# A place of its own for the mixed tokens of the keys, and an earlier mixture for batch 0

## The chip, the cores and the metric

The kernel runs on one core of a Trainium2 chip. Its time is the device time of one execution, in microseconds. The profile comes from one execution that the hardware profiler recorded.

## The reference

Three layers follow each other, all in float32, for 4 batches of 576 tokens.

1. Attention with 8 heads of 64 columns. The scores are causal; beside q.k/8 they get a bias from s: with cum the running sum of max(s, 0), query i and key j get min(cum[j] - cum[i], 0). Then softmax, and the product with v.
2. A feed-forward layer on the attention's output x (512 columns), with token mixing:

```python
xk = mu_k * x + (1.0 - mu_k) * x_prev      # x_prev: the token before
xr = mu_r * x + (1.0 - mu_r) * x_prev
k = np.maximum(xk @ w_k, 0.0)              # 512 -> 1024
v = k * k @ w_v                            # 1024 -> 512
r = 1.0 / (1.0 + np.exp(-(xr @ w_r)))
x = r * v
```

3. A token and channel mixer with w_tok1, w_tok2, w_ch1 and w_ch2, whose weights and work begin late in the kernel; the change does not touch it.

The weights come in float64.

## The kernel before, in words

**Products.** Most products are made from pairs: each operand is split in a high part, a float32 copy rounded to the faster matrix format, and a low part, the rest. `products` then issues three matrix products for each piece of 128 rows (high x high, high x low, low x high). Tokens and weights all have such pairs.

**Weights.** A float64 weight is loaded as two 32-bit words. `weight_split` (lines 567 to 577) rebuilds a float32 from them with two ScalarE steps (a copy of the high words, an integer scaling of the low ones) and two VectorE steps (shift-or, and-or); ScalarE then copies the high part into the weight's tile, and the low part is a subtraction, on GpSimd for w_k and w_r, on VectorE for w_v. For w_v (half=1) another ScalarE pass multiplies the float32 by 0.5 in place, ahead of the copy: the gate is made as 0.5 (1 + tanh), and this half is put into the weight. The first twelve pieces are w_k (8) and w_r (4), each of 512 KB; their raw tiles come from the pool `wst` (five buffers). w_v comes in 16 pieces of 256 KB, whose raw tiles are borrowed from the six buffers of `xt`, the pool of the attention's outputs.

**Attention of batch 0.** The first 256 queries of each head are done by `early` (two tiles of 128 queries per head, lines 311 to 340), the rest by `late` (three tiles, lines 358 to 385) and `late_pv`. A step is: scores on TensorE, the negated row maximum on VectorE (L261), the exponential on ScalarE (L271), normalising on GpSimd (L274), transposes on TensorE, a copy of them on ScalarE, the product with v. After every second head, the outputs of the pair of heads are copied into `xt[0, p]` by VectorE (line 340). Between the early tiles and in the first late heads `keep_busy` issues products whose result nobody uses; their PSUM tile is one of the two of the pool that `up` uses as well. Batches 1 to 3 follow as visits (`scores`, `transposes`, `values`).

**The feed-forward layer.** `mix(b, c, i, p)` (lines 472 to 481) mixes the tokens of chunk c (0: the first 256, 1: the other 320) for one pair of heads: a scaled copy into a temporary (L478), the other token added (L479), both on VectorE, the high part on ScalarE (L480), the low part on VectorE (L481). i=0 writes XK, i=1 XR. `up` (lines 483 to 493) makes one of eight blocks of k from XK and w_k, then relu and two squares on ScalarE into a temporary and into KK, and the low part on GpSimd (L493). `gate` reads XR, `down` reads KK.

**What sets the order.** Nothing is issued in program order. Each block of code has a place, a number given by `at(place)`; smaller places go first. A planner simulates the engines and writes for each engine a fixed list: whenever an engine is free, the instruction that is ready and has the smallest place. On the chip each engine takes its list in order and waits where something is not ready. The SP, ACT and GpSimd queues also issue the DMAs, in the same manner. Early head h, tile j has place 2h + j; the n-th late step has 16 + n; a feed-forward unit that belongs to step n has 16 + n + 3. The twelve weight splits have places 1.6, 2.8 and so on to 14.8, the w_v pieces 18, 19.5 and so on. The mixes of batch 0's first chunk for XK have place 16, and the mu loads (`mixes`) place 9.

**Memory.** Pools on the left side lie like a stack. First `wst` (raw weight tiles) and `cp` (the early heads' inputs, tiles and the bias) are opened; after both are closed in the program, `act` (XK, XR, KK) and `sm` (the temporaries t and e, three each) take the same memory. A tile may be written once all tiles that lay there before are no longer used. `bias_rows` (lines 164 to 180) makes the running sum of s into `cum`; `split_bias` (lines 182 to 193) writes it, split in pairs, to DRAM (ext_d) in three chunks through one tile `e`; `late_load` reads it back for the late heads.

## Time and profile before

| | |
|---|---|
| time, median of 3 runs | 890.04 us (888.98 to 893.41) |
| the profiled execution | 887.59 us, of which the span is 885.8 us |
| TensorE (PE) busy in the span | 847.3 us |
| VectorE (DVE), ScalarE (ACT), GpSimd (POOL) busy | 535.2, 469.8, 347.9 us |
| mean granted clock of TensorE | 0.982 of full speed |

Times in the rows are microseconds from the start of the span. PE is the matrix product, PEld the load of its stationary operand; L110 is line 110 of the kernel. A busy engine is one that has an instruction in it. "Out <- in" names the tiles. In the views of waits the left side waited for the right one. A granted clock of 1.00 is 2.4 GHz, 0.50 is 1.2 GHz.

### The profile page before, as it was taken

To read this page: it belongs to the slowest core of one execution; us is meant where nothing else is said; L and a number is where in the kernel's file an instruction comes from. 1 tells how busy PE (TensorE), PEld (TensorE's weight loads), DVE (VectorE), ACT (ScalarE), POOL (GpSimd) and SP (SyncE) were. 2 spreads that over 40 slices of the span, in tenths; PEclk is the share of its full clock that TensorE was granted. 3 is DMA by queue.
4 is the path that set the end of the run, shared out by engine and by line. 5 is a ranking of instruction groups with operands and counts; after the bars stand their busy time and mean duration, and the time that the engine had idled before them with its cause. 6 is when DMAs were issued, how large, how long until landed. Compare 5 with 4: busy or idle time off the path is not lost.

```text
span 885.8 us, 17817 instructions
## 1 busy us (share of the span) xinstructions
PE 847.3 (96%) x6185; PEld 793.4 (90%) x6185; DVE 535.2 (60%) x1583; ACT 469.8 (53%) x1320; POOL 347.9 (39%) x510
## 2 busy tenths in 40 slices
PE   7969999999789999999989899999999999999998
PEld 5736677998679999999989899899999999999998
DVE  4896897677899677996657866871331322222321
ACT  3877976866776765868456775760320211211210
POOL 3676876877773433645244674650000000000000
PEclk8969999999999999999999999999999999999999
DMA  7975667578753334441132656653022112112100
GB/s 195 255 207 170 205 188 215 163 215 245 199 159 85 82 79 107 100 121 48 50 100 80 206 157 197 208 186 124 25 71 63 44 40 66 38 42 67 43 25 24
DMA packets 78730, 108.37 MB, mean 122 GB/s; under 512 B 11072, under 2 KB 59200, under 8 KB 78640
## 3 DMA queue, kind: packets, MB, share of 16 engines
q1 hardware_dynamic: 68352, 77.40, 32.0%
q0 software_dynamic: 8416, 29.24, 10.2%
q8 instruction: 49, 0.80, 0.4%
q10 hardware_dynamic: 1872, 0.59, 0.4%
q14 instruction: 41, 0.34, 0.1%
HBM read 77.74 MB, written 28.90 MB: 120 GB/s over the span
## 4 chain that ended last, share of the span: by engine, by line
PE 70%; DVE 9%; DMA 7%; ACT 5%; issue 4%; POOL 3%; SPq 0%; ACTq 0%; POOLq 0%; DVEq 0%
PE c L110 32%; PE vd L110 8%; PE h L110 7%; PE r L110 4%; PE t L110 3%; PE t L411 3%; PE pv L463 3%; DMA hl_d<-qkp 2%; DMA raw<-in_moe_w_ch_dram 2%; DVE raw L572 2%; PE s L286 2%; PE pv L397 2%; PE s L287 2%; DVE raw L573 1%; PE s L368 1%
## 5 line engine op out<-in xcount | busy, mean ns | idle before, releaser
L813 ACT ACTIVATE HID<-c 128x256 fp32r<-128x256 f32 (+1 forms) x96 | 39.4, 410 | 218.7 <-PE c L110 218.5
L274 POOL TENSOR_SCALAR P<-P,sum 64x576 f32<-64x576 f32 (+4 forms) x160 | 101.2, 636 | 94.1 <-DVE sum L273 41.9
L110 PE MATMUL h<-XK,WK 128*128 128x256 f32 (+1 forms) x768 | 124.5, 302 | 4.1 <-ACT k L490 2.0
L110 PE MATMUL vd<-KK,WV 128*128 128x256 f32 (+1 forms) x768 | 121.6, 300 | 0.0
L110 PEld LDWEIGHTS h<-XK,WK 128*128 128x128 f32 x768 | 106.6, 188 | 10.1 <-ACT k L490 3.1
L271 ACT ACTIVATE P<-P,mx 64x576 f32<-64x576 f32 (+4 forms) x160 | 95.9, 600 | 28.5 <-DVE mx L261 27.5
L110 PEld LDWEIGHTS vd<-KK,WV 128*128 128x128 f32 x768 | 106.8, 188 | 1.7 <-issue 0.7
L110 PE MATMUL c<-U,WK 128*128 128x256 f32 (+1 forms) x768 | 102.6, 291 | 2.1 <-DVE HID L814 2.1
L110 PE MATMUL c<-HID,WV 128*128 128x256 f32 (+1 forms) x768 | 104.4, 291 | 0.0
L110 PEld LDWEIGHTS c<-U,WK 128*128 128x128 f32 x768 | 98.7, 188 | 2.4 <-DVE HID L814 2.3
L110 PEld LDWEIGHTS c<-HID,WV 128*128 128x128 f32 x768 | 100.4, 188 | 0.0
L814 DVE SCALAR_TENSOR_TENSOR HID<-c,HID 128x256 fp32r<-128x256 f32 (+1 forms) x96 | 43.9, 457 | 83.3 <-ACT HID L813 83.2
L878 DVE TENSOR_TENSOR ut<-c,ut 128x256 f32<-128x256 f32 (+1 forms) x32 | 14.7, 458 | 119.9 <-PE c L110 112.5
L261 DVE CUSTOM_DVE_ANT_0 P<-s,maskc 64x288 f32<-64x288 f32 (+4 forms) x160 | 74.9, 474 | 16.9 <-PE idle L155 4.4
L493 POOL TENSOR_TENSOR KK<-k,KK 128x256 fp32r<-128x256 f32 (+1 forms) x64 | 53.5, 837 | 34.7 <-ACT k L492 29.2
L110 PE MATMUL r<-XR,WR 128*128 128x320 f32 (+1 forms) x384 | 61.4, 302 | 2.6 <-ACT k L490 2.6
L75 ACT ACTIVATE raw<-raw 128x256 f32<-128x256 f32 (+2 forms) x101 | 46.8, 466 | 29.4 <-DMA raw<-in_moe_w_ch_dram 9.7
L572 DVE SCALAR_TENSOR_TENSOR raw<-raw 128x256 int32<-128x256 int32 (+2 forms) x85 | 49.7, 584 | 19.8 <-ACT raw L571 16.6
L110 PEld LDWEIGHTS r<-XR,WR 128*128 128x128 f32 x384 | 53.9, 192 | 3.6 <-ACT k L490 2.9
L411 PE MATMUL t<-ident,P 128*128 128x128 f32 (+1 forms) x360 | 52.8, 262 | 3.5 <-DVE PT L440 2.4
L110 PE MATMUL c<-HID,WR 128*128 128x256 f32 (+1 forms) x384 | 54.5, 291 | 0.0
L573 DVE SCALAR_TENSOR_TENSOR raw<-raw 128x256 int32<-128x256 int32 (+2 forms) x85 | 52.9, 624 | 1.2
(116 smaller groups left out, 1695.9 us busy)
## 6 DMA issues: line engine op xcount, KB each, us to landing
X<-hl_d SPq DMA_DIRECT2D x72, 288.0 KB
hl_d<-qkp POOLq DMA_DIRECT2D x48, 288.0 KB, 4.2
raw<-in_moe_w_ch_dram POOLq DMA_DIRECT2D x48, 256.0 KB, 3.7
qkr<-in_qk_dram SPq DMA_DIRECT2D x48, 144.0 KB
yt<-y_d SPq DMA_DIRECT2D x16, 288.0 KB
u_d<-yt SPq DMA_DIRECT2D x16, 288.0 KB
raw<-in_moe_w_k_dram SPq DMA_DIRECT2D x8, 512.0 KB
raw<-in_moe_w_v_dram SPq DMA_DIRECT2D x16, 256.0 KB
```

The costliest lines, as they stand in the source:

```text
L75: nc.scalar.activation(out=out, in_=in_, func=AF.Copy, scale=scale)
L110: nc.tensor.matmul(ps, a, b, start=first and i == 0, stop=last and i == n - 1)
L261: nc.vector.tensor_tensor_reduce(out=P[0:m, c0:c1], in0=ps[0:m, 0:c1 - c0], in1=maskc[0:m, 512 - q0 + c0:512 - q0 + c1], scale=-scale, sca ...
L271: nc.scalar.activation(out=P[0:m, 0:w], in_=P[0:m, 0:w], func=AF.Exp, bias=mx[0:m, x:x + 1], scale=-1.0, accum_out=sm[0:m, 0:1])
L274: nc.gpsimd.tensor_scalar(out=P[0:m, 0:w], in0=P[0:m, 0:w], scalar1=sm[0:m, 1:2], scalar2=1.0, op0=ALU.mult, op1=ALU.mult)
L411: nc.tensor.transpose(ps[0:r, p0 + m * k:p0 + m * k + m], P[0:m, 128 * k:128 * k + r], ident[0:m, 0:m])
L463: nc.tensor.matmul(ps[:, o:n], vv[:, k, :], part, start=(k == 0 and t == 0), stop=(k == nk - 1 and t == len(parts) - 1),)
L493: nc.gpsimd.tensor_tensor(out=kk[:, 1, m, 0:n], in0=t[:, 0:n], in1=f32(kk[:, 0, m, 0:n]), op=ALU.subtract)
L572: nc.vector.scalar_tensor_tensor(out=low, in0=high, scalar=3, in1=low, op0=ALU.logical_shift_left, op1=ALU.bitwise_or)
L573: nc.vector.scalar_tensor_tensor(out=low, in0=high, scalar=-2 ** 31, in1=low, op0=ALU.bitwise_and, op1=ALU.bitwise_or)
L813: nc.scalar.activation(out=hi, in_=ps, func=AF.Relu)
L814: nc.vector.scalar_tensor_tensor(out=lo, in0=ps, scalar=0.0, in1=f32(hi), op0=ALU.max, op1=ALU.subtract)
```

## The change

XK gets a pool of its own, opened ahead of `wst`, so that it shares memory with nothing. To make room, `wst` has three buffers and not five, `cum` is computed in place of `st`, and the bias goes to DRAM in four chunks of 144 columns and not three of 192. The four mixes of batch 0's first chunk for XK are placed behind the early heads 1, 3, 5 and 7 (places 3.9, 7.9, 11.9 and 15.9) and use one temporary of 256 columns in `cp`; the mu loads get place 3. The in-place half of w_v is gone: the copy of the high part multiplies by 0.5, and the low part is one VectorE step, 0.5 times the float32 less the high part.

```diff
--- before.py
+++ after.py
@@ -165,7 +165,7 @@
         st = cp.tile([G, S], F32, name="st")
         nc.sync.dma_start(out=st, in_=s)
         e32 = cp.tile([G, 2, 2, QC], F32, name="e32")
-        cum = cp.tile([G, S], F32, name="cum")
+        cum = st
         nc.gpsimd.memset(e32[:, 0, 0, :], 1.0)
         nc.gpsimd.memset(e32[:, 1, 1, :], 1.0)
         for c, (a, z) in enumerate(CHS):
@@ -180,7 +180,7 @@
         return cum, e32
 
     def split_bias(cp, cum):
-        n = 3
+        n = 4
         for c in range(n):
             a, z = S * c // n, S * (c + 1) // n
             e = cp.tile([G, 4, 2, z - a], F32R, name="e")
@@ -474,7 +474,7 @@
         x = xt[b, p]
         a, z = CHS[c]
         n = z - a
-        t = act["sm"].tile([128, CM], F32, tag="t", name="t", bufs=3)
+        t = act["mt"].tile([128, act["mtw"]], F32, tag="t", name="t", bufs=act["mtb"])
         nc.vector.tensor_scalar(out=t[:, 0:n], in0=x[:, 1 + a:1 + z], scalar1=mu[:, i, p:p + 1], scalar2=1.0, op0=ALU.mult, op1=ALU.mult)
         nc.vector.scalar_tensor_tensor(out=t[:, 0:n], in0=x[:, a:z], scalar=omu[:, i, p:p + 1], in1=t[:, 0:n], op0=ALU.mult, op1=ALU.add)
         nc.scalar.activation(out=dst[:, 0, p, 0:n], in_=t[:, 0:n], func=AF.Copy)
@@ -571,10 +571,11 @@
         nc.scalar.activation(out=low.bitcast(U32), in_=low.bitcast(U32), func=AF.Copy, scale=TOP3, bias=-0.496)
         nc.vector.scalar_tensor_tensor(out=low, in0=high, scalar=3, in1=low, op0=ALU.logical_shift_left, op1=ALU.bitwise_or)
         nc.vector.scalar_tensor_tensor(out=low, in0=high, scalar=-2 ** 31, in1=low, op0=ALU.bitwise_and, op1=ALU.bitwise_or)
+        copy("A", hi, f32(low), 0.5 if half else 1.0)
         if half:
-            copy("A", f32(low), f32(low), 0.5)
-        copy("A", hi, f32(low))
-        (nc.vector if half else nc.gpsimd).tensor_tensor(out=lo, in0=f32(low), in1=f32(hi), op=ALU.subtract)
+            nc.vector.scalar_tensor_tensor(out=lo, in0=f32(low), scalar=0.5, in1=f32(hi), op0=ALU.mult, op1=ALU.subtract)
+        else:
+            nc.gpsimd.tensor_tensor(out=lo, in0=f32(low), in1=f32(hi), op=ALU.subtract)
 
     def rows(sw, k0, k1):
         r0 = 128 * k0
@@ -668,7 +669,9 @@
     nc.vector.memset(maskc, 0.0)
     act["idle"] = ps_d.tile([128, 512], F32, tag="d", name="idle")
     keep_busy(13, maskc, 512)
-    wst_s, sp = open_pool(name="wst", bufs=5)
+    xk_s, xk_p = open_pool(name="xk", bufs=1, reuse_waits="tile")
+    act["XK"] = xk_p.tile([128, 2, KD, CM], F32R, name="XK")
+    wst_s, sp = open_pool(name="wst", bufs=3)
     cp_s, cp = open_pool(name="cp", bufs=1)
     cum, e32 = bias_rows(cp)
     early_at.append((cp.tile([128, 8 * QC], F32, name="HL"), 0, 4))
@@ -694,17 +697,21 @@
         for y in range(4, 8):
             early_bias(y, e32)
 
+    act["mt"], act["mtb"], act["mtw"] = cp, 1, QC
     constants()
+    with at(3):
+        mixes()
     for h in range(H):
         if h == 1:
             after_bias()
         for j in range(2):
             with at(2 * h + j):
                 early(h, j, V0, cp)
+        if h % 2 == 1:
+            with at(2 * h + 1 + 0.9):
+                mix(0, 0, 0, h // 2)
     with at(2):
         split_bias(cp, cum)
-    with at(9):
-        mixes()
     with at(N0 - 5):
         for h in range(4):
             late_load(h)
@@ -723,10 +730,10 @@
     wst_s.close()
 
     ap_s, ap = open_pool(name="act", bufs=1, reuse_waits="tile")
-    act["XK"] = ap.tile([128, 2, KD, CM], F32R, name="XK")
     act["XR"] = ap.tile([128, 2, KD, CM], F32R, name="XR")
     act["KK"] = ap.tile([128, 2, KF, CM], F32R, name="KK")
     st_s, act["sm"] = open_pool(name="sm", bufs=2, reuse_waits="tile")
+    act["mt"], act["mtb"], act["mtw"] = act["sm"], 3, CM
     x = 18
     for f in range(0, DM, 128):
         for k in range(0, KF, 2):
@@ -734,9 +741,6 @@
                 weight_load((k, f), rows(w_v, k, k + 2)[:, :, f:f + 128], S // 2, xt_p, "xt")
                 weight_split((k, f), wv[:, 0, k:k + 2, f:f + 128], wv[:, 1, k:k + 2, f:f + 128], 1)
             x += 1.5
-    with at(N0):
-        for p in range(KD):
-            mix(0, 0, 0, p)
     todo = {}
     base = (NS - 2) * H
     starts, ends = [0, 2, 4, 4], [2, 4, 4, 4]
@@ -910,6 +914,7 @@
     run(fill)
     st_s.close()
     ap_s.close()
+    xk_s.close()
     ch_p = ctx.enter_context(tc.tile_pool(name="ch", bufs=1, reuse_waits="tile"))
     U = ch_p.tile([128, 2, KD, CH], F32R, name="U")
     HID = ch_p.tile([128, 2, KC, CH], F32R, name="HID")
```

## Rows read from the trace of the kernel before

**Rows 1.** The page: the span, and busy time of each engine

```profile
span 885.8 us, 17817 instructions
...
PE 847.3 (96%) x6185; PEld 793.4 (90%) x6185; DVE 535.2 (60%) x1583; ACT 469.8 (53%) x1320; POOL 347.9 (39%) x510
```

**Rows 2.** Times by stretch: from:to, length, busy us, PEclk, DMA share, GB/s

```profile
20.00:50.00 30.00, 29.13 (x192) 22.42 (x190) 25.24 (x75) 26.48 (x66) 20.85 (x25) 1.00 0.99 263
50.00:72.00 22.00, 14.38 (x59) 7.51 (x59) 18.58 (x42) 15.24 (x40) 16.87 (x17) 0.69 0.56 170
72.00:100.00 28.00, 26.43 (x157) 18.49 (x158) 21.59 (x64) 22.05 (x68) 18.62 (x25) 1.00 0.62 190
100.00:150.00 50.00, 50.00 (x319) 37.50 (x318) 41.92 (x123) 38.04 (x111) 36.72 (x52) 1.00 0.70 203
```

**Rows 3.** Times by stretch, 53 to 65 us in steps of 4 us

```profile
53.00:57.00 4.00, 1.45 (x9) 0.84 (x8) 4.00 (x9) 4.00 (x11) 2.36 (x3) 0.50 0.87 222
57.00:61.00 4.00, 1.43 (x2) 0.28 (x2) 4.00 (x5) 2.70 (x8) 3.65 (x4) 0.50 0.26 90
61.00:65.00 4.00, 3.47 (x5) 1.25 (x6) 3.96 (x15) 1.76 (x4) 1.83 (x2) 0.50 0.70 215
```

**Rows 4.** Waits of TensorE, 50 to 72 us: total us, times, longest

```profile
PE s L368 <- DVE mx L261: 7.2, 3, 3.1
PE t L377 <- ACT PT L75: 0.7, 1, 0.7
PE h L110 <- ACT XK L480: 0.4, 1, 0.4
```

**Rows 5.** Timeline (start, us, engine, line, operation): last weight split, first XK

```profile
69.11 1.29 POOL L577 TENSOR_TENSOR WR<-raw,WR 128x512 fp32r<-128x512 f32 x1
...
70.95 1.01 ACT L480 ACTIVATE XK<-t 128x256 fp32r<-128x256 f32 x3
...
71.40 1.11 PE L110 MATMUL h<-XK,WK 128*128 128x256 f32 x4 [0.41 <-ACT XK L480]
```

**Rows 6.** The mix's lines, 40 to 82 us: ns min/median/max, first and last

```profile
L478 DVE TENSOR_SCALAR t<-xt,mu x4: 338/342/1377, 53.6 to 73.0; 128x256 f32<-128x256 f32 x4
...
L479 DVE SCALAR_TENSOR_TENSOR t<-xt,omu,t x4: 467/474/1014, 57.3 to 74.3; 128x256 f32<-128x256 f32 x4
...
L481 DVE TENSOR_TENSOR XK<-t,XK x4: 405/414/419, 71.4 to 78.2; 128x256 fp32r<-128x256 f32 x4
```

**Rows 7.** Timeline: scores and pv of TensorE at either clock

```profile
61.53 2.07 PE L368 MATMUL s<-X 68*128 68x512 f32 x2 [3.10 <-DVE mx L261]
...
63.53 3.50 PE L397 MATMUL pv<-PT,VV 128*64 128x320 f32 x10
...
73.94 1.02 PE L368 MATMUL s<-X 68*128 68x512 f32 x2
...
74.89 2.41 PE L397 MATMUL pv<-PT,VV 128*64 128x320 f32 x10
```

**Rows 8.** Timeline, 38 to 58 us: weight pieces on four engines

```profile
47.21 2.60 DVE L572 SCALAR_TENSOR_TENSOR raw<-raw 128x512 int32<-128x512 int32 x1 [0.60 <-ACT raw L571]
...
51.43 0.46 SPq L559 DMA_DIRECT2D raw<-in_moe_w_r_dram  x1
...
52.05 0.68 ACT L75 ACTIVATE raw<-raw 128x512 f32<-128x512 f32 x1 [1.40 <-DMA raw<-in_moe_w_r_dram]
...
53.88 0.68 DVE L573 SCALAR_TENSOR_TENSOR raw<-raw 128x512 int32<-128x512 int32 x1
...
54.64 1.33 POOL L577 TENSOR_TENSOR WR<-raw,WR 128x512 fp32r<-128x512 f32 x1 [1.83 <-ACT WR L75]
```

**Rows 9.** The instructions of line 491, 70 to 100 us

```profile
L491 ACT ACTIVATE KK<-k x5: 399/409/425, 83.1 to 99.2; 128x256 fp32r<-128x256 f32 x5
```

**Rows 10.** Waits of the SP queue, 0 to 100 us

```profile
SPq L354 <- DMA ext_d<-e: 6.1, 1, 6.1
```

**Rows 11.** Line 75's copies that write raw, 0 to 140 us

```profile
L75 ACT ACTIVATE raw<-raw x44: 422/443/687, 14.1 to 134.5; 128x256 f32<-128x256 f32 x32, 128x512 f32<-128x512 f32 x12
```

## The prediction

> **What bounds the kernel now.** I read the page first: TensorE is busy for 847.3 us of a span of 885.8 us [rows 1], so a change can win only what lies in the 38.5 us in which it is idle, or in stretches where its clock is low. The times by stretch say where an early change can bite [rows 2]: from 50 to 72 us TensorE has 14.38 us of work in 22 us, at a mean granted clock of 0.69, while VectorE is busy for 18.58 us. In the stretches behind it TensorE is the bound (26.43 of 28 us, then 50.00 of 50 us), with VectorE at 21.59 and 41.92 us. Cut finer, VectorE is full from 53 to 65 us and TensorE's clock is at 0.50, the 1.2 GHz level, with 1.45, 1.43 and 3.47 us of work in three times 4 us [rows 3]. The clock fell after TensorE had gone idle and rose again when its work came back. The view of the waits names the reason for the idleness: 7.2 us of three scores waiting for the row maximum on VectorE, 0.7 us for a transposed tile on ScalarE, and 0.4 us for the first product of the keys waiting for XK [rows 4]. The last is small, but it is the one that matters: between 49 and 71 us TensorE has no filler. The eight `up` units of batch 0 have place 19 on, so by their places they belong between the scores that wait at 51 to 61 us, and the first starts at 71.40 us [rows 5]. XK is first written at 70.95 us, half a microsecond after the last split of w_r has let go of its raw tile (POOL, 69.11 + 1.29 us) [rows 5]: XK lies where the raw weight tiles lay.
>
> **The layout, worked out from the code.** Per partition a raw tile is 512 x 2 x 4 = 4,096 B and XK 2 x 4 x 320 x 4 = 10,240 B. Before: five raw tiles (0 to 20,480), then the early pool; after these close, XK takes 0 to 10,240 (raw tiles 1 to 3), XR 10,240 to 20,480, KK 20,480 on (early pool only). After: XK 0 to 10,240 alone, three raw tiles 10,240 to 22,528, then the early pool; XR lies on the raw tiles, and KK, from 20,480, now shares 2,048 B with the third raw tile. So XK is freed, and KK gets the wait: squares of `up` can't be written before the twelfth weight piece, the last in the third raw tile, is split.
>
> **Part by part.**
> 1. *XK free, four mixes earlier.* Each mix is two VectorE steps (0.34 and 0.47 us), one ScalarE copy (three took 1.01 us in a row [rows 5]) and one VectorE subtraction (0.41) [rows 6], no DMA. Those of pairs 0 to 2 now follow early heads 1, 3 and 5, so 3 x 1.22 = 3.7 us of VectorE and 1.0 us of ScalarE move from 53 to 78 us to before 50 us, where VectorE has 25.24 us of 30 [rows 2]. They push what is queued behind them (weight splits, row maxima of late head 0) by 0 to 3.7 us, and take the same away from 53 to 61 us, where VectorE is full [rows 3]. Net 0. Pair 3's mix stays where it is, behind early head 7 (the first mix step starts at 53.6 us before, the last subtraction at 78.2 [rows 6]), so XK is whole at about 57 us in place of 78.
> 2. *Filler for TensorE.* What can be won is the idle time of rows 4, 7.2 + 0.7 + 0.4 = 8.3 us, and the slow clock. Two scores of 512 columns took 2.07 us at the low level and 1.02 us at the high one, ten pv products 3.50 and 2.41 us [rows 7]; the 6.35 us of work between 53 and 65 us [rows 3] would shrink by 2.0 us (at 3.50/2.41) to 3.2 us (at one half). I take 2.5, so 10.8 us in all. Lower end: only the gap after 57 us, 3.1 + 0.4 = 3.5 us, with the clock still low.
> 3. *What the next stretch gives back.* 10.8 us of products done before 72 us leave 26.4 - 10.8 = 15.6 us of TensorE's work in the 28 us that follow. VectorE has 21.59 us there, less four subtractions and one mix's two steps that are already done (1.6 + 0.8): 19.1 us. VectorE becomes the bound; at the full occupancy of 53 to 61 us that is 19 us, at nine tenths 21 to 22 us. The stretch can shrink by 6 to 7 us, not by 10.8; the rest comes back as idle time. Behind 100 us TensorE is full with VectorE at 84% [rows 2], so what was won is carried to the end. Value taken: 5.5 us.
> 4. *Three raw tiles for five.* The load of the last w_r piece is issued at 51.43 us, when the fifth piece before it is released, and ScalarE already waits 1.40 us for a w_r piece that was asked for earlier [rows 8]. With three tiles that load waits for the third piece before it, split at 54.64 + 1.33 = 55.97 us [rows 8], 4.5 us later. w_r itself is needed only by the gates far behind 100 us, so this costs nothing through w_r; through KK it is a limit at about 70.4 + 4.5 = 75 us. The first square stands at 83.1 us before [rows 9], and until then three temporary tiles and the PSUM tile hold four `up` units, 48 products, about as many as fill the gaps. Cost taken 0; ends 0 and +12 us (each of the three earlier turns slips by 4 us too).
> 5. *Bias in four chunks, sums in place of `st`.* One more round of four memsets, four small VectorE steps, and a landing on the ACT queue. SP once waited 6.1 us for such a landing [rows 10], ahead of the late heads' inputs. One more could delay the first late scores by up to that, or by nothing, as two weight loads fewer are then in flight. The early heads cover it: TensorE has 29.13 us of work in the 30 us from 20 to 50 us [rows 2]. I take 0; without that cover it is 6.
> 6. *w_v's half in its copies.* 16 ScalarE passes of 128x256 at the 0.44 us median of that group [rows 11] go: 7.0 us, from 40 to 135 us. The subtraction becomes a three-operand step: 0.47 for 0.41 us [rows 6], so +1 us in 16 on VectorE; the ends are 0 and, at 1.01, +9.6 us. ScalarE rarely ends last for TensorE; 0.5 us gain.
> The mu loads and the one small step on them stand at the head of their queues already; moving their place changes nothing.
>
> Sum: 5.5 + 0.5 = 6.0 us. Against the profiled execution (887.59 us, span 885.8) that is 881.6; that execution is 2.4 us under the median of 890.04, and I give the time in terms of the median: 884.
>
> **A rule that speaks against it.** A VectorE step with two inputs in SBUF stands still beside GpSimd here: one 128x512 shift-or took 2.60 us while GpSimd was normalising and subtracting, another 0.68 us [rows 8]. The Trainium skill, "SBUF — State Buffer", section "Who interferes with whom", says why: such a VectorE step and a GpSimd step that reads SBUF exclude each other for a whole instruction. The trace agrees (2.60 against 0.68). The mixes that move have two such steps each. At this pair's difference, 1.92 us, six of them would cost VectorE 11.5 us and the time would be some 4 us over B's, 894; by the mixes' own rows it is the 3.2 us of B.
>
> **Rivals.**
> *A. All of it is won.* The packed order finds enough filler (gates, down products) after 72 us: 890 - 11 = 879. For it: TensorE at 50.00 of 50 us behind 100 us. Against: w_v's pieces and the gates' inputs are VectorE work.
> *B. Given back on VectorE.* The six two-input steps of the early mixes fall between 22 and 45 us, where GpSimd is busy for 20.85 of 30 us [rows 2]. At L479's longest, 1.01 for 0.47 us [rows 6], each loses 0.54 us, 3.2 us in all; with the 3.7 us of part 1, VectorE is 7 us late at 50 us, all maxima behind it too, and the gap that is to be filled grows by what the filling wins: 890. The same time comes if the order puts `up` no earlier though XK is free (the change then doesn't do what it says).
> *C. KK waits at the head of ScalarE's queue.* Now squares come early, at about 62 us (57, twelve products and the queue), but KK is shut until the last w_r piece is split, 75 to 82 us. ScalarE runs in order: the exponentials queued behind a square wait 13 to 20 us, and with them GpSimd's normalising, the transposes and pv. Filler of at most four units covers 10 of it; loss 3 to 10 us, with slower weight pieces feeding it. I take 7: 897. It decides from the point where ScalarE sits idle more than 10 us between 60 and 82 us until POOL's last split. Against: the squares are placed behind splits that have earlier places, so the order should not put a square ahead of its release by much.
>
> **How the numbers follow.** Forecast (6 us, own range 880.5 to 887.5): 0.42. A: 0.13. B: 0.27. C: 0.18. The range goes from 877.5, a little past A, to 894, past B and half the way to C's 897; it leaves out under 2 in 10. What can be told from no change is 0.5%, 4.45 us, so faster is under 885.6: A and most of the forecast, 0.51; within, B and the forecast's upper end: 0.30; slower: 0.19.
>
> **What would show it.** Right: first `up` product at 50 to 60 us in place of 71.4; granted clock 1.00 between 55 and 65 us; idle waits of rows 4 under 4 us; VectorE or ScalarE over nine tenths from 70 to 95 us; `up` and late head 3 finished about 6 us earlier; the rest of the trace the same, shifted. Wrong: XK's first write early but the first `up` still near 70 us (B); scores of late head 1 later than 56 and 61 us (B); ScalarE idle ahead of a square (C); w_r's last split behind 80 us (C); a new gap behind 200 us, where I expect only a shift.

## The result, and the profile after

The changed kernel takes 898.59 us (median of 7 runs, 896.76 to 902.49), the kernel before on the same chip 890.61 (7 runs, 888.98 to 895.89). The ratio is 1.0086, with a 95% interval of 1.0063 to 1.0108: slower by about 8 us, 14.6 us over the forecast and 4.6 over the upper end of its range. The profiled execution of the changed kernel has a span of 897.0 us, 11.2 more than before [rows 1]. It is near its kernel's median (898.75 us in all), while the profiled execution of the kernel before lies 3.0 us under its own (887.59 against 890.61). So about 3 of the 11.2 us, and up to 3 us of every lag given below, belong to that one execution.

The page of the changed kernel, span and busy time (answers to [rows 1]):

```profile
span 897.0 us, 17829 instructions
...
PE 854.2 (95%) x6185; PEld 797.5 (89%) x6185; DVE 536.2 (60%) x1587; ACT 465.4 (52%) x1304; POOL 351.4 (39%) x514
```

TensorE has the same 6185 products. They take 6.9 us longer in sum and the rest, 4.3 us, is idle time; VectorE has hardly more to do than before.

The changed kernel by the stretches of [rows 2] (from:to, length, busy us of PE, PEld, DVE, ACT and POOL, granted clock, DMA share, GB/s):

```profile
20.00:50.00 30.00, 27.36 (x173) 20.20 (x171) 24.70 (x82) 22.57 (x62) 18.02 (x26) 1.00 0.87 226
50.00:72.00 22.00, 18.04 (x88) 10.71 (x85) 18.80 (x41) 16.38 (x41) 14.26 (x16) 0.84 0.59 174
72.00:100.00 28.00, 23.35 (x120) 14.16 (x119) 23.17 (x62) 20.98 (x60) 23.77 (x25) 0.88 0.70 212
100.00:150.00 50.00, 46.71 (x280) 34.91 (x279) 39.96 (x100) 32.52 (x96) 35.51 (x48) 0.93 0.57 170
```

From 50 to 72 us it went the way that was forecast: 18.04 us of work in place of 14.38, the mean granted clock 0.84 in place of 0.69. Then more than that is given back: 23.35 for 26.43 us from 72 to 100, 46.71 for 50.00 behind that, at 0.88 and 0.93 where the clock had been 1.00. Over these stretches no engine is full: VectorE stands at 83% and 80%, GpSimd at 85% and 71%.

The changed kernel in the stretches of [rows 3]:

```profile
53.00:57.00 4.00, 2.77 (x21) 1.98 (x19) 4.00 (x2) 1.84 (x4) 3.96 (x5) 1.00 0.21 74
57.00:61.00 4.00, 1.54 (x4) 0.69 (x4) 4.00 (x12) 2.23 (x7) 2.22 (x3) 0.77 0.41 133
61.00:65.00 4.00, 4.00 (x7) 1.37 (x6) 3.84 (x13) 2.92 (x8) 1.64 (x3) 0.50 1.07 281
```

What TensorE waited for in the changed kernel (total us, times, longest), from 50 to 72 us (answers to [rows 4]) and then from 84 to 112 us:

```profile
PE s L368 <- DVE mx L261: 4.0, 3, 2.8
...
PE s L368 <- DVE mx L261: 4.6, 3, 3.0
PE t L377 <- POOL P L274: 0.9, 1, 0.9
```

and over the whole of the late heads, 50 to 160 us, before and then after:

```profile
PE s L368 <- DVE mx L261: 7.5, 4, 3.1
```

```profile
PE s L368 <- DVE mx L261: 10.8, 7, 3.0
```

The scores' wait for the row maximum shrank where the change aimed at it (7.2 to 4.0 us) and came back at 84 to 112 us, and the sum grew from 7.5 to 10.8 us. This sum alone is not the price of the change: a kernel of the next section (e_xr) that is over 4 us faster than the kernel before waited longer in the same stretch:

```profile
PE s L368 <- DVE mx L261: 9.1, 4, 3.2
PE t L377 <- POOL P L274: 3.2, 3, 1.5
```

What is left of the wait from 50 to 72 us can be read from the changed kernel's timeline. One step of w_v's low part, the three-operand step that the change wrote, took 4.59 us on VectorE while GpSimd was busy for 3.96 of the 4 us from 53 to 57; another took 0.39 us. The row maximum comes behind it in VectorE's list, and TensorE waits 2.77 us for that maximum:

```profile
53.42 4.59 DVE L576 SCALAR_TENSOR_TENSOR WV<-raw,WV 128x256 fp32r<-128x256 f32 x1
57.94 0.54 DVE L261 CUSTOM_DVE_ANT_0 P<-s,maskc 128x384 f32<-128x384 f32 x1
...
63.06 0.39 DVE L576 SCALAR_TENSOR_TENSOR WV<-raw,WV 128x256 fp32r<-128x256 f32 x1
```

```profile
58.54 0.70 PE L368 MATMUL s<-X 68*64 68x288 f32 x2 [2.77 <-DVE mx L261]
```

What became of XK and the first products (the timeline of the changed kernel; answers to [rows 5]):

```profile
29.42 0.42 ACT L480 ACTIVATE XK<-t 128x256 fp32r<-128x256 f32 x1
...
63.31 0.40 ACT L480 ACTIVATE XK<-t 128x256 fp32r<-128x256 f32 x1
...
31.65 0.60 PE L110 MATMUL h<-XK,WK 128*128 128x256 f32 x3
40.93 0.81 PE L110 MATMUL h<-XK,WK 128*128 128x256 f32 x3
51.24 0.79 PE L110 MATMUL h<-XK,WK 128*128 128x256 f32 x3
68.64 0.60 PE L110 MATMUL h<-XK,WK 128*128 128x256 f32 x3
72.55 1.65 PE L110 MATMUL h<-XK,WK 128*128 128x256 f32 x12
```

XK is free at once, as read from the layout. But the first `up` unit goes with the pairs, three products for each, and its last three come at 68.64 us, behind pair 3's mix at 63.31 us and not at 57; the second unit starts at 72.55. The first square into KK stands at 93.7 us (83.1 before, [rows 9]), behind the last split of w_r, which starts at 90.92.

A line that both traces give: lag. The matrix products of an execution are put in order of time, each with the duration that its kind takes undisturbed (the 20th percentile over all the executions), and summed. The lag is the time at which a kernel has done the share of this work that the kernel before had done at a given moment, less that moment (us; negative: ahead). Single entries hold to about 1.5 us; they depend on how products that overlap are counted.

```
time before   25     45     60     85    110    200    260    300    end
after        2.5    2.9   -5.7   -3.0   10.4    8.4   14.8   11.6   11.3
```

So 5.7 us ahead at 60 us, the way that was forecast; 10.4 us behind at 110; then another 6 us lost and half of them won back between 200 and 300 us; nothing behind that.

### The profile page after: what moved, and what is told of

The parts are those of the page before. It is cut to its first block, busy times and chain, and to the rows that moved or that the text cites. A ratio compares the mean times of both kernels' runs of the same rounds, so it can differ in the third digit from the quotient of the medians.

```text
span 897.0 us, 17829 instructions
## 1 busy us (share of the span) xinstructions
PE 854.2 (95%) x6185; PEld 797.5 (89%) x6185; DVE 536.2 (60%) x1587; ACT 465.4 (52%) x1304; POOL 351.4 (39%) x514
## 4 chain that ended last, share of the span: by engine, by line
PE 74%; DVE 9%; DMA 6%; ACT 4%; issue 3%; POOL 3%; SPq 0%; ACTq 0%; DVEq 0%; POOLq 0%
PE c L110 32%; PE vd L110 9%; PE h L110 8%; PE r L110 5%; PE t L411 4%; PE pv L463 4%; PE t L110 3%; PE s L286 2%; PE s L287 2%; DMA raw<-in_moe_w_ch_dram 2%; DVE raw L572 2%; PE pv L397 2%; PE s L368 2%; DVE raw L573 1%; DMA ext_d<-e 1%
## 5 line engine op out<-in xcount | busy, mean ns | idle before, releaser
L274 POOL TENSOR_SCALAR P<-P,sum 64x576 f32<-64x576 f32 (+4 forms) x160 | 104.0, 654 | 109.2 <-DVE sum L273 49.6
L110 PE MATMUL h<-XK,WK 128*128 128x256 f32 (+1 forms) x768 | 127.6, 308 | 2.8 <-DVE XK L481 1.1
L110 PE MATMUL vd<-KK,WV 128*128 128x256 f32 (+1 forms) x768 | 118.2, 298 | 0.0
L110 PEld LDWEIGHTS h<-XK,WK 128*128 128x128 f32 x768 | 110.1, 195 | 8.5 <-ACT PT L75 1.4
L882 DVE TENSOR_TENSOR ut<-c,ut 128x256 f32<-128x256 f32 (+1 forms) x32 | 14.6, 458 | 119.7 <-PE c L110 112.4
L261 DVE CUSTOM_DVE_ANT_0 P<-s,maskc 64x288 f32<-64x288 f32 (+4 forms) x160 | 74.6, 473 | 15.9 <-PE idle L155 5.1
L572 DVE SCALAR_TENSOR_TENSOR raw<-raw 128x256 int32<-128x256 int32 (+2 forms) x85 | 53.8, 634 | 21.3 <-ACT raw L571 17.7
L75 ACT ACTIVATE raw<-raw 128x256 f32<-128x256 f32 (+2 forms) x85 | 40.0, 471 | 27.0 <-DMA raw<-in_moe_w_ch_dram 9.6
L110 PE MATMUL c<-U,C1A 128*128 128x256 f32 (+1 forms) x384 | 52.8, 296 | 0.0
```

The costliest lines, as they stand in the source:

```text
L75: nc.scalar.activation(out=out, in_=in_, func=AF.Copy, scale=scale)
L110: nc.tensor.matmul(ps, a, b, start=first and i == 0, stop=last and i == n - 1)
L261: nc.vector.tensor_tensor_reduce(out=P[0:m, c0:c1], in0=ps[0:m, 0:c1 - c0], in1=maskc[0:m, 512 - q0 + c0:512 - q0 + c1], scale=-scale, sca ...
L274: nc.gpsimd.tensor_scalar(out=P[0:m, 0:w], in0=P[0:m, 0:w], scalar1=sm[0:m, 1:2], scalar2=1.0, op0=ALU.mult, op1=ALU.mult)
L572: nc.vector.scalar_tensor_tensor(out=low, in0=high, scalar=3, in1=low, op0=ALU.logical_shift_left, op1=ALU.bitwise_or)
```

## The experiments

Ratios are to the kernel before on the same chip, with 95% intervals. The expectations number their theories: 1, three raw tiles, and so late weight pieces, cost the time; 5, the wait for KK costs it; 7, the fourth round of the bias; 8, products of the keys that are done early are only taken from later gaps.

**Parts alone.** Three raw tiles (theory 1):

```diff
-    wst_s, sp = open_pool(name="wst", bufs=5)
+    wst_s, sp = open_pool(name="wst", bufs=3)
```

> The kernel before with three raw weight tiles in place of five and nothing else. Theory 1 (three raw tiles make the first twelve weight pieces late, and what lies on those tiles with them): the last w_r piece, split by 70.4 us before and by 92.2 us after, is split at 80 to 92 us here, and the time is 895 to 903 us. Rival 2 (the four early mixes on VectorE cost the time) and rival 3 (the fourth round of the bias holds the SP queue): the split comes at about 75 us and the time is 889 to 893 us.

886.11 us, 0.9943 (0.9921 to 0.9966): faster, though w_r's last split went from 69.11 to this:

```profile
81.51 1.29 POOL L577 TENSOR_TENSOR WR<-raw,WR 128x512 fp32r<-128x512 f32 x1
```

Theory 1 falls for this part alone: the split came when the theory said (80 to 92 us), and the time did not follow. The bias in four chunks (theory 7):

```diff
-        cum = cp.tile([G, S], F32, name="cum")
+        cum = st
...
-        n = 3
+        n = 4
```

> The kernel before with the running sum in place of st and the bias in four chunks; nothing else. Theory 1 and rival 2: 889 to 892 us, since the early heads cover the extra landing. Rival 3: 893 to 898 us, with the first read of ext_d later than 31.3 us and the late scores behind it.

895.36 us, 1.0050 (1.0031 to 1.0068). The fourth chunk has to wait until the third has left the one tile that all chunks go through; VectorE stands for 6.8 us in front of a small cast, and with it the row maxima of the early heads, for which ScalarE then waits:

```profile
DVE e L77 <- DMA ext_d<-e: 6.8, 1, 6.8
...
ACT P L271 <- DVE mx L261: 7.6, 2, 6.6
```

The half of w_v in its copies:

```diff
+        copy("A", hi, f32(low), 0.5 if half else 1.0)
         if half:
-            copy("A", f32(low), f32(low), 0.5)
-        copy("A", hi, f32(low))
-        (nc.vector if half else nc.gpsimd).tensor_tensor(out=lo, in0=f32(low), in1=f32(hi), op=ALU.subtract)
+            nc.vector.scalar_tensor_tensor(out=lo, in0=f32(low), scalar=0.5, in1=f32(hi), op0=ALU.mult, op1=ALU.subtract)
+        else:
+            nc.gpsimd.tensor_tensor(out=lo, in0=f32(low), in1=f32(hi), op=ALU.subtract)
```

> The kernel before with w_v's half put into its copies; nothing else. Theory 1, and the prediction: 888 to 891 us (16 ScalarE passes of 0.44 us less, of which little ends last). Rival 4 (any edit changes the planner's lists, and the lists alone move the time): as well 3 to 6 us above or below 890.

882.77 us, 0.9905 (0.9879 to 0.9931): the best kernel of the study, and it beats the kernels before and after. The changed kernel without the early mixes:

```diff
-        if h % 2 == 1:
-            with at(2 * h + 1 + 0.9):
-                mix(0, 0, 0, h // 2)
...
+    with at(N0):
+        for p in range(KD):
+            mix(0, 0, 0, p)
```

> The changed kernel with batch 0's four mixes at place 16 again, as before; XK keeps its own memory, three raw tiles stay. Rival 2: with the early mixes gone the time returns to 889 to 893 us. Theory 1: 896 to 902 us, w_r's last split still behind 85 us, as the mixes are not what makes the weights late.

892.43 us, 1.0020 (0.9997 to 1.0042). The three parts alone make 0.9943 x 1.0050 x 0.9905 = 0.990. With XK in its own memory besides it is 1.002, with the early mixes 1.0086. What costs must be in these two, or in the way the parts meet.

**The wait for KK.** The changed kernel with `sm` laid so that the temporaries t and KK lie clear of the raw tiles:

```diff
-    act["KK"] = ap.tile([128, 2, KF, CM], F32R, name="KK")
+    se_s, act["se"] = open_pool(name="se", bufs=2, reuse_waits="tile")
     st_s, act["sm"] = open_pool(name="sm", bufs=2, reuse_waits="tile")
+    kk_s, kk_p = open_pool(name="kk", bufs=1, reuse_waits="tile")
+    act["KK"] = kk_p.tile([128, 2, KF, CM], F32R, name="KK")
...
-        e = act["sm"].tile([128, CM], F32, tag="e", ...
+        e = act["se"].tile([128, CM], F32, tag="e", ...
```

> The changed kernel with only the places of three tiles moved: KK and the temporaries t lie on the memory of the early pool alone, the gates' temporaries e lie on the third raw tile. Theory 5 (the loss between 85 and 110 us is KK shut behind the last w_r piece, so that no fifth up unit can run between 84 and 99.7 us): the first square comes before 80 us, up units go on without that gap, the low clock of 92 to 102 us is gone, and the time falls by 6 to 12 us, to 887 to 893 us. Theory 6 (the late weight pieces and the mixes load VectorE and ScalarE there, KK does not matter): 896 to 900 us.

898.43 us, 1.0079 (1.0046 to 1.0112). The first square comes 21 us earlier (first and last start in the line):

```profile
L491 ACT ACTIVATE KK<-k x4: 400/404/409, 72.6 to 109.7; 128x256 fp32r<-128x256 f32 x4
```

and the time is the same: theory 5 falls, and rival C's mechanism with it, though its 897 came nearest.

**Three chunks, first try.** The changed kernel, and the one with KK free, with the bias in three chunks; the room was made by letting the mixes' temporary share the early heads' ring of tiles E1:

```diff
-        n = 4
+        n = 3
...
-    act["mt"], act["mtb"], act["mtw"] = cp, 1, QC
+    act["mt"], act["mtb"], act["mtw"], act["mtag"] = cp, 2, QC, "E1"
```

> The changed kernel with the bias in three chunks again (to make room the early mixes' temporary shares the early heads' second tile of 256 columns). Theory 7 (the fourth round puts a VectorE and a GpSimd step, both waiting for the landing of the third chunk, ahead of row maxima: 4.5 us at 19.9 to 24.4 us): the wait is gone, TensorE's work is 2.5 to 3.5 us earlier from 25 us on, and the time falls by 2 to 5 us, to 893 to 897 us. If the loss at 85 to 110 us swallows it (theory 5 alone): 897 to 900 us.

> Both mends in the changed kernel: KK off the raw tiles, and the bias in three chunks. Theories 5 and 7 together: 883 to 889 us, under the kernel before. Theory 6: 893 to 899 us.

904.52 us, 1.0143 (1.0106 to 1.0179), and 902.01, 1.0121 (1.0087 to 1.0156). Both say nothing of the bias: in a shared ring the early heads have to wait for mixes (by the layout), and TensorE has 22.50 and 23.95 us of work from 20 to 50 us in place of the changed kernel's 27.36.

**An order alone.** The kernel before with w_v's pieces placed from 17.4 on and not 18; the planner writes another order of the same instructions:

```diff
-    x = 18
+    x = 17.4
```

> The kernel before with the w_v pieces placed from 17.4 on in place of 18 and nothing else, which changes some of the lists' order and no work. Rival 4 (lists alone move the time by several microseconds, so the 8 us that the half in the copies won are order and not work): 2 to 6 us above or below 890.8 us. Against it: 889.5 to 892 us.

888.73 us, 0.9964 (0.9937 to 0.9992). An order by itself is worth 0.4% here, and the pairs of orders further down differ by 0.2 to 0.5%; effects of that size need more than one pair.

**Three chunks, and four kernels around a free XK.** The changed kernel with three chunks (the room comes from a shorter ring of the small tile `sum`); that without early mixes; the kernel before with w_v's half and three raw tiles; and the kernel before with w_v's half and its first two pools exchanged, so that XK lies on the early heads' tiles and is free some 12 us sooner (first written at 59.5 us, 71.2 without the exchange), with five raw tiles (KK moves behind the temporaries for that):

```diff
-        n = 4
+        n = 3
...
-        sm = st_p.tile([128, 2], F32, tag="sum", name="sum")
+        sm = st_p.tile([128, 2], F32, tag="sum", name="sum", bufs=5)
```

> The changed kernel with the bias in three chunks and all else kept (32 B come from one buffer less of the small sums). Theory 7 with three raw tiles (the fourth round delays the first weight split, 25.6 for 20.4 us, and with three raw tiles each of the four turns of loads behind it): the first split is back at 20 to 21 us, the last one before 84 us in place of 92, time 885 to 892 us. Theory 8 (the early mixes only let TensorE borrow filler that is missing at 85 to 110 us): the loss there stays, 894 to 899 us.

> XK in its own memory, three raw tiles, w_v's half in its copies, but the mixes at place 16 and the bias in three chunks. Theory 7: 879 to 886 us. If the parts only add up (892.4 less the 4.5 us of the fourth round): 887 to 889 us. If XK's own memory is itself what costs: 890 us or more.

> The kernel before with the two parts that were faster alone: w_v's half in its copies (0.9905) and three raw tiles (0.9943). If they add up: 0.985, 876 to 880 us. If what they won is the order of the lists: anywhere between 881 and 890 us.

```diff
-    wst_s, sp = open_pool(name="wst", bufs=5)
     cp_s, cp = open_pool(name="cp", bufs=1)
+    wst_s, sp = open_pool(name="wst", bufs=5)
...
-    act["KK"] = ap.tile([128, 2, KF, CM], F32R, name="KK")
     st_s, act["sm"] = open_pool(name="sm", bufs=2, reuse_waits="tile")
+    kk_s, kk_p = open_pool(name="kk", bufs=1, reuse_waits="tile")
+    act["KK"] = kk_p.tile([128, 2, KF, CM], F32R, name="KK")
```

> The kernel before with w_v's half in its copies and the two early pools exchanged, so that XK, XR and the temporaries lie on the early heads' memory (free at about 53 us) and KK partly on the raw tiles; five raw tiles, three chunks, mixes at place 16. If an XK that is free at 53 us is worth what the prediction said: 3 to 6 us under w_v's half alone (882.8), 876 to 880 us. Theory 8 (filler is borrowed): 881 to 886 us.

898.87 us, 1.0068 (1.0043 to 1.0093); 898.17, 1.0063 (1.0038 to 1.0088); 887.87, 0.9955 (0.9936 to 0.9975); 890.42, 0.9980 (0.9956 to 1.0004). With three chunks the wait at 20 us is gone, TensorE is 1.8 us ahead at 45 us and 8.6 at 60, the most of all, and the kernel ends where the changed one does: theory 7 explains the changed kernel's first 50 us and not its end. The early mixes cost nothing here. Freeing XK costs in both pairs: 1.0063 against 0.9955, and 0.9980 against 0.9905 for w_v's half alone. Nor do the parts add up: beside w_v's half, three raw tiles cost 0.5% (0.9955 against 0.9905), where alone they won 0.6%; and with XK free and the mixes late, the kernel with the fourth chunk is the faster one (1.0020 against 1.0063).

**The same memory, XK late.** The kernel of 898.17 us with one exchange:

```diff
-    act["XK"] = xk_p.tile([128, 2, KD, CM], F32R, name="XK")
+    act["XR"] = xk_p.tile([128, 2, KD, CM], F32R, name="XR")
...
-    act["XR"] = ap.tile([128, 2, KD, CM], F32R, name="XR")
+    act["XK"] = ap.tile([128, 2, KD, CM], F32R, name="XK")
```

> The kernel changed with its mixes at place 16 and the bias in three chunks (898.2 us when it was timed), with one exchange: XR takes the place of its own, XK lies on the raw tiles as in the kernel before. The memory in use is the same, byte for byte; only XK comes free late again. Theory 8 (early products of the keys spend the filler that later gaps need): first XK write back near 85 us, first h near 86, time 885 to 891, as of the kernel before with three raw tiles and w_v's half in its copies (887.9). Rival, the layout with a further pool costs it (other addresses, other waits for memory): 895 to 900. Rival, nothing but the order's luck: anything, with no relation to XK.

886.62 us, 0.9939 (0.9916 to 0.9962), against 1.0063 with XK free: a factor of 1.0125 (0.0034 either way, the two intervals' half-widths added in squares). XK is written at 83.20 us and `up` starts at 84.25. The stretches show what was exchanged (from 60 to 84 and 84 to 112 us; this kernel, then its partner with XK free, the changed kernel, and the one before). The partner's profiled execution took 890.49 us, 7.7 under its median, so its trace shows a mild case.

```profile
60.00:84.00 24.00, 14.87 (x67) 8.11 (x67) 16.87 (x43) 16.57 (x42) 18.29 (x20) 0.86 0.59 183
84.00:112.00 28.00, 28.00 (x150) 18.86 (x151) 23.11 (x68) 21.95 (x67) 17.93 (x25) 0.94 0.61 177
```

```profile
60.00:84.00 24.00, 20.03 (x118) 14.51 (x117) 21.81 (x46) 18.01 (x45) 20.57 (x18) 0.93 0.55 165
84.00:112.00 28.00, 24.19 (x109) 13.93 (x107) 21.62 (x62) 18.94 (x59) 17.44 (x23) 0.88 0.52 155
```

```profile
60.00:84.00 24.00, 23.57 (x119) 14.76 (x120) 19.28 (x53) 19.82 (x51) 15.19 (x17) 0.87 0.81 241
84.00:112.00 28.00, 21.59 (x94) 12.14 (x93) 21.06 (x55) 18.26 (x53) 22.17 (x24) 0.82 0.55 166
```

```profile
60.00:84.00 24.00, 21.64 (x110) 13.35 (x111) 15.64 (x53) 14.98 (x42) 15.25 (x18) 0.88 0.58 175
84.00:112.00 28.00, 26.75 (x158) 18.14 (x157) 23.13 (x64) 26.00 (x83) 22.39 (x30) 1.00 0.60 182
```

The kernel with XK late leaves 9.1 us empty from 60 to 84 us, more than the change set out to fill, and then has none empty; the changed kernel is full first and leaves 6.4 us empty after, the partner 4.0 and 3.8. VectorE, from 72 to 100 us, differs more (XK late, then free; the stretch, and the shift-or of w_v's pieces in it):

```profile
72.00:100.00 28.00, 25.29 (x126) 16.52 (x125) 20.01 (x61) 19.46 (x56) 18.02 (x23) 0.88 0.55 164
...
L572 DVE SCALAR_TENSOR_TENSOR raw<-raw 128x256 int32<-128x256 int32 x5 | 3.2, 638 | 2.0 <-ACT raw L571 2.0
```

```profile
72.00:100.00 28.00, 25.17 (x130) 16.24 (x130) 26.44 (x61) 21.78 (x64) 21.55 (x24) 0.88 0.59 171
...
L572 DVE SCALAR_TENSOR_TENSOR raw<-raw 128x256 int32<-128x256 int32 x5 | 6.2, 1236 | 0.1
```

VectorE's 61 instructions of the stretch keep it busy for 20.01 us in the one and 26.44 of 28 us in the other. They are not quite the same steps, but equal ones are longer too: five shift-ors of w_v's pieces took 638 ns in the mean with XK late and 1236 with XK free.

**The pair under other orders.** The pools exchanged without w_v's half, the pool diff above on the kernel before:

> The kernel before with its first two pools exchanged, so that XK lies on the early heads' tiles and comes free some 15 us earlier, with five raw tiles and w_v's half as before. With that half in its copies this exchange cost 0.75 per cent (890.4 against 882.8). Theory 8: XK from about 58 us, 893 to 899, over the kernel before by 0.3 to 0.9 per cent, the loss behind 95 us. Prediction's step 2 and 3: 882 to 888. Order's luck: between 885 and 898 without relation.

891.96 us, 1.0003 (0.9983 to 1.0024). And the kernels of 898.17 and 887.87 us, with a free and a late XK, under another order:

```diff
-            x += 1.5
+            x += 1.0
```

> The kernel changed with its mixes at place 16 and the bias in three chunks (898.2), XK free early, and w_v's pieces 1.0 places apart in place of 1.5: the same instructions in another order. It measures what an order alone is worth. Theory 8: within 3 us of 898, and over its partner with XK on the raw tiles by 5 to 12 us. Order's luck: the two partners differ by less than 3 us, or the other way round.

> The kernel before with three raw tiles and w_v's half in its copies (887.9), XK late, and w_v's pieces 1.0 places apart in place of 1.5: the partner of the run before. Theory 8: 885 to 891. Order's luck: anything from 883 to 898.

892.23 us, 1.0012 (0.9985 to 1.0038), and 890.62, 0.9990 (0.9967 to 1.0013). The free one is still not faster, but the cost is 0.2% and inside the intervals. TensorE's lag shows the exchange in the plainest form:

```
time before            25     45     60     85    110    200    260    300    end
XK free, e_ordfree   -0.5   -1.2   -4.9   -3.1    4.4    1.9    8.4    5.6    4.0
XK late, e_ordraw     0.0   -0.7   -4.8    6.4    5.8    6.0    7.3    4.5    6.4
XK free, e_n3b       -0.7   -1.8   -8.6    1.3    9.0   12.0   13.7   10.4    9.9
XK late, e_xr        -0.3   -1.0   -5.6    5.7    5.0    3.3    3.6   -0.3   -1.0
```

At 85 us the free kernel of the first pair is 9.5 us ahead of its partner; at 110 us 1.4. In the second pair 4.4 us ahead have become 4.0 behind. (e_ordraw's profiled execution is 3 us above its own median; its lag is too high by that. In the second pair e_n3b, which has the early mixes too, stands for e_xr's partner, whose trace is of a fast execution.)

The free XK also moves the end of the late heads, read here from where their last score starts (the last start of line 368, us):

| XK late, free | last late score | ratio, free to late |
|---|---|---|
| e_xr, e_laten3 | 124.6, 138.3 | 1.0125 |
| e_wvb3, e_laten3 | 125.4, 138.3 | 1.011 |
| e_wv, e_swapwv | 128.5, 134.1 | 1.008 |
| e_ordraw, e_ordfree | 125.9, 130.7 | 1.002 |
| before, e_swap | 130.7, 133.5 | 1.000 |

In every pair the late heads end later with XK free, by 2.8 to 13.7 us, and the pairs stand in the same order by this delay as by their loss. The kernels before and after have 130.7 and 136.5, and 131.4 and 143.4 in the order of the next paragraph. Each start is from one execution, so this is a sign of where the loss arises and not a proof.

**Before and after under a third order.** Both with one more product on the unused tile at the start, where TensorE waits anyway:

```diff
-    keep_busy(13, maskc, 512)
+    keep_busy(14, maskc, 512)
```

> The changed kernel with 14 in place of 13 products on an unused tile at the very start, where TensorE waits for its first input anyway (13 of them took 4.48 us from 1.25 us, and the first score came at 6.52 us): it costs under 0.5 us by itself, but the planner starts from another moment and writes another order. If the loss is in the change (XK free early, whatever the order), 894 to 902; if it is mainly the luck of the order, anything from 883 to 902, and within 4 us of its partner, the kernel before with 14.

> The kernel before with 14 in place of 13 products at the start, the partner of the run before it. If the order is of little weight, 889 to 893; by the runs so far (an order alone moved one kernel by 0.36, one by 0.31 and one by 0.66 per cent) it may lie anywhere from 884 to 897. The ratio of the two partners is a second measurement of the change under an order of its own.

900.70 us, 1.0134 (1.0084 to 1.0184), and 891.67, 1.0023 (0.9995 to 1.0051). Their ratio is 1.011 (0.0057 either way, as above): the change loses under both orders that were tried, and not only under the one that the planner happened to write first.

## Why the prediction was wrong

**The step that failed** is the end of part 3: "Behind 100 us TensorE is full with VectorE at 84%, so what was won is carried to the end." TensorE got its lead (5.7 us at 60 us; part 2 had 10.8 by 72, part 3 kept 5.5), and none of it was carried. The late heads wait for row maxima, and filling that wait with products of the keys does not make the maxima come sooner. It takes the products away from the next late heads, which wait for maxima in the same way; before, the 96 products came just there (71.4 to 106.5 us) and hid it. Full at 100 us meant that filler was there, not that TensorE was the bound for whatever is moved. Runs with a late and a free XK under the same remaining parts show the exchange from both sides (9.5 us of lead down to 1.4; 14.87 and 28.00 us of work in the two stretches against 20.03 and 24.19).

A term of part 3 failed with it: VectorE's 19.1 us from 72 to 100 us. The changed kernel has 23.17 there, as three shift-ors of 512 columns and their followers, from w_k's and w_r's pieces, have slipped into the stretch (none was there before), and in the pair it is 26.44 us with XK free and 20.01 with XK late. So the maxima did not come sooner, and the late heads ended later.

In no comparison does the free XK win: +1.25 and +1.1% (the same free kernel against two partners), +0.8, +0.2 and 0.0%.

Why it ends in a loss and not at nothing stays open. The changed kernel has nearly its whole lag at 110 us (10.4 of 11.3). In the pair of e_n3b and e_xr it lies mostly behind: they are 4.0 us apart at 110 us, 8.7 at 200 and 10.9 at the end; and from 160 to 200 us TensorE has 36.58 us of work in e_laten3 and 40.00 in e_xr:

```profile
160.00:200.00 40.00, 36.58 (x256) 34.25 (x255) 30.47 (x104) 31.41 (x93) 29.44 (x44) 1.00 0.69 178
```

```profile
160.00:200.00 40.00, 40.00 (x285) 38.38 (x284) 28.11 (x109) 32.13 (x95) 33.37 (x47) 1.00 0.75 214
```

Three things go with the loss: late heads that end later, VectorE steps that take longer, and products at a lower granted clock (0.82 from 84 to 112 us in the changed kernel, 1.00 before). No run parts them. How much of a given pair's loss is the planner's order (0.2 to 0.5% for an order alone, and 0 to 1.25% for the same exchange under different orders) stays open too.

Along one path the steps are: w_v's half, three raw tiles and a pool for XR, 0.9939; XK in that pool in place of XR, 1.0125; early mixes, 1.0005; the fourth bias chunk, 1.0018. Each is the quotient of two measured neighbours, so their product is 1.0086 by construction: it divides the loss and does not test it. By another path the early mixes cost 0.66% (1.0086 against 1.0020, with four chunks) and the chunk 0.50% (alone). What a part is worth depends on what it meets, so the terms below are for their own trials.

Point by point:

1. *Mixes, net 0.* Held with three chunks (1.0068 with them, 1.0063 without), not with four (1.0086 and 1.0020). The same lag, taken over VectorE's steps in the changed kernel, is within 1 us of nothing at 60 us. XK whole at 57 us was wrong: pair 3 was mixed at 63.31. The mixes' two-input step beside GpSimd grew little in the median (483 ns; one of five took 1442), so rival B's price was not paid by the mixes. The rule behind it was: by w_v's step of 4.59 us, which part 6 had at 0.47 us and at most 1.01. (The prediction's 0.68 us for "another" shift-or is the and-or of L573, of the same size; and it gave no working for the 4 us that 11.5 us of standing would add to B's time.)

```profile
L479 DVE SCALAR_TENSOR_TENSOR t<-xt,omu,t x5: 468/483/1442, 28.5 to 75.3; 128x256 f32<-128x256 f32 x5
```

2. *Filler.* Right in place, half in size: the wait from 50 to 72 us went from 8.3 to 4.0 us, of which 2.77 are behind the step of 4.59 us; the clock was 1.00, 0.77 and 0.50 in the three times 4 us that were to be at 1.00.
3. *Half given back on VectorE.* The engine was right, the size wrong, as above: VectorE was busy for 22.43 of the 25 us from 70 to 95 us (17.58 before), and more than the lead was given back.
4. *Three raw tiles, 0.* The delay was mis-sized: w_r's last split ended at 82.80 us alone, 12.4 later than before and not 4.5, and at 92.20 in the changed kernel. The time did not follow: -4.7 us alone, as w_r is not needed earlier and later weight pieces may stand less in the way (my reading; no run parts it from the order, and beside w_v's half the same edit costs 0.5%). KK's wait was there, and taking it away won nothing.
5. *Fourth bias chunk, 0 (6 without cover).* Mis-sized: +4.6 us alone (with XK free and the mixes late, the sign is the other one). The cover was TensorE's 29.13 us of 30; but the wait stands on VectorE, ahead of the early heads' maxima. In the changed kernel it is 4.5 us, and TensorE's 27.36 of 30 us show it:

```profile
24.41 0.31 DVE L77 CAST e<-st 32x144 fp32r<-32x144 f32 x1 [4.51 <-DMA ext_d<-e]
```

6. *w_v's half, 0.5 us.* Mis-sized: 8.0 us alone (0.95%, of which an order may be a part). The 16 passes went as counted, 44 to 28 [rows 11]:

```profile
L75 ACT ACTIVATE raw<-raw x28: 421/452/692, 13.7 to 126.0; 128x256 f32<-128x256 f32 x16, 128x512 f32<-128x512 f32 x12
```

ScalarE ends few waits, but every step of a late head passes through its queue, and I priced only the waits that it ends last (my reading again).

Of the tests that were named: first `up` between 50 and 60 us, no (31.65, and a whole unit only by 68.64); the clock at 1.00, no; waits under 4 us, no (4.0); VectorE over nine tenths from 70 to 95 us, just under (0.90); `up` and late head 3 six us earlier, no (the last product of the first chunk's `up` at 121.3 us in place of 106.5). Of the signs of being wrong: w_r's last split behind 80 us (C), yes, but ScalarE did not wait ahead of a square, and C's 897, the nearest time, was luck; "a new gap behind 200 us, where I expect only a shift", yes: from 240 to 260 us TensorE has 14.92 us of work in place of 18.75. Before, then after:

```profile
240.00:260.00 20.00, 18.75 (x148) 17.35 (x146) 18.79 (x69) 18.57 (x59) 16.55 (x26) 1.00 0.69 182
```

```profile
240.00:260.00 20.00, 14.92 (x88) 12.76 (x87) 16.94 (x65) 14.58 (x44) 13.26 (x21) 0.84 0.82 208
```

## What to carry to other kernels

Work that fills an engine's gap is worth its length only if the engine is the bound from there on; where every step of a chain opens the same gap, ask which later gap the moved work used to fill, and follow the wait over the whole chain, not in its first stretch. A resource that is "full" with filler is not a bound. Price an engine's steps in the company that the change gives them: the same step took 0.39 and 4.59 us here. Where a planner writes the order, measure an order alone (here 0.2 to 0.5%) before an effect of that size is put down to a part, and repeat the pair under a second order; and test the parts of a bundled change one by one, since here two of them won 0.6 and 0.95% alone, the two together 0.45%, and the bundle lost 0.9%.

## What the runs showed of the hardware

A VectorE step with a single input took 4.10 us where 0.34 us is usual for it [rows 6]. VectorE's timeline in the kernel with KK clear of the raw tiles, and GpSimd's in the same stretch:

```profile
94.15 4.10 DVE L478 TENSOR_SCALAR t<-xt,mu 128x256 f32<-128x256 f32 x1 [3.59 <-POOL KK L493]
...
94.08 1.98 POOL L274 TENSOR_SCALAR P<-P,sum 128x512 f32<-128x512 f32 x3
96.03 0.78 POOL L224 TENSOR_TENSOR qkp<-qkr,qkp 128x288 f32<-128x288 f32 x1
96.78 1.28 POOL L578 TENSOR_TENSOR WR<-raw,WR 128x512 fp32r<-128x512 f32 x1
```

It stood through five GpSimd steps, 94.08 to 98.06 us, and ended 0.2 us after them. The prediction had looked for this in steps with two inputs alone; the Trainium skill, "SBUF — State Buffer", section "Who interferes with whom", counts `tensor_scalar` among the steps that can take the port shared with GpSimd, and the trace agrees (4.10 against 0.34 us).

With the fourth bias chunk a small write to DRAM was waited for. The third chunk's write (144 KB) was issued at 17.15 us in e_n4 and at 17.06 in the changed kernel, among weight loads of 512 KB, and VectorE's next cast into the tile started at 26.22 and 24.41 us: it had waited 6.8 and 4.5 us for the landing. SP waited 7.1 us for a landing of that kind in the changed kernel (6.1 before, [rows 10]).
